# A planned attention and gated-MLP kernel: weight conversion in PSUM, staggered units, and drawn visit orders

## Chip, cores and metric

One core of one Trainium2 chip. The metric is the device time of one execution in microseconds, the median of several runs. Five engines matter: PE (TensorE), DVE (VectorE), ACT (ScalarE), POOL (GpSimd) and SP, which issues the DMAs. PEld is the weight load of PE.

## The reference

Attention for 8 batches of 8 heads, 576 tokens, head size 64, in which only scores close to the row's maximum count, and behind it a gated MLP on 4608 tokens:

```python
scores = scale * np.matmul(q, k.transpose(0, 1, 3, 2))
thresh = np.max(scores, axis=-1, keepdims=True) - tau
scores = np.where(scores >= thresh, scores, -1000000000.0)
attn = np.exp(scores - np.max(scores, axis=-1, keepdims=True))
attn = attn / (np.sum(attn, axis=-1, keepdims=True) + 1e-09)
x = np.matmul(attn, v)                 # to 4608 x 512, all fp32
gate = 1.0 / (1.0 + np.exp(-(x @ w_gate)))
out = (gate * (x @ w_val)) @ w_out     # d_ff 1536
```

## The kernel before

**A planner writes the order.** The program records operations (`Plan.op`: engine, cost, key, what is read and written). `Plan.run` then plays them with these costs: on each free engine it starts the ready operation with the smallest key for which buffers are free, and emits instructions in the order so found. Each engine runs its list in that order; nothing is reordered on the chip. The costs decide the order and nothing else.

**Attention.** 32 visits, one for each batch and pair of heads (named 0_0 to 7_3). A visit has nine score tiles of 128 rows. For each (`tile_steps`): PE writes 128x576 scores into PSUM (L623, two row halves of the array at once), DVE takes the row maximum (L630), ACT the exponential (L644), DVE masks and sums (L647), PE transposes (L738, `Group.transpose`), ACT copies the transposed tile to SBUF (L686). `outputs` multiplies by V (L777, column halves of the array).

**PSUM.** Eight banks, shared out by the planner (`PLACES`, `SLOTS`). A buffer of tag "s" takes a pair of banks: scores, transposes, leftover keys, V products. A buffer of tag "b" takes one bank: accumulators of the MLP. Once the MLP runs beside attention, "s" buffers are kept to three pairs (`homes`), and at most two accumulators are alive (`MOE_CAP`).

**Weights.** `convert` is called 36 times for 128x512 pieces. A piece arrives as pairs of 32-bit words and becomes one fp32 word and then a rounded high and a low part: POOL keeps the sign bits (L497, `wa`), ACT scales the magnitude (L501, `wb`), DVE shifts and joins `wb` with `wa` (L504), DVE joins the low word with `wb` (L510), ACT rounds (L522), POOL subtracts (L528). `wb` is one SBUF buffer (tag "cv", one slot).

**MLP.** Block 0 (batch 0) runs with the whole array (`whole_units`, L888). Blocks 1 and 2 (batches 1 and 2) run in `in_units`: for each of 12 column tiles f the accumulators of the gate (i = 0) and of the value (i = 1) are summed together, one on array rows 0 to 63 and the other on rows 64 to 127 (`phase`, L848), and then with the rows exchanged. Between the two phases ACT reads one element of an accumulator (`seen`, L857), which keeps both row halves from adding to one bank at once. After the second phase ACT takes tanh (L956) and DVE forms the product (L961). Then come `out_pair` (L848 again, operands `gpp`, prepared on ACT, POOL and DVE) and, once the attention's buffers are free, three rounds of `in_two` (L1179) and `out_two` (L1321) for the other six blocks, with the whole array.

Of the kernel before, what the change touches and what calls it, by code (L numbers as in the profile page):

```python
# [10 lines left out]
F32 = mybir.dt.float32  # L11
# [32 lines left out]
class Plan:  # L44
# [5 lines left out]
    def __init__(self, pools, slots):  # L50
        self.pools, self.slots = pools, slots
        self.ops, self.held, self.made, self.given = [], {}, {}, {}
        self.live = {}

    def buf(self, tag, shape, dtype, name, cls=None):
        return Buf(self, tag, shape, dtype, name, cls)
# [9 lines left out]
    def op(self, eng, cost, key, emit, reads=(), writes=(), also=(), leave=0, behind=None, after=(), lag=0.0, mode="full"):  # L66


        o = Op()
        o.eng, o.cost, o.emit, o.key, o.leave, o.lag = eng, cost, emit, key, leave, lag  # L70
        o.succ, o.seq, o.ready, o.mode = [], len(self.ops), 0.0, mode
        deps, bufs = set(after), []
        for group, write in ((reads, False), (writes, True)):
            for x in group:
                b, part = x if isinstance(x, tuple) else (x, None)
                for q, p, w in b.accesses:
                    if (write or w) and (p is None or part is None or p == part):
# [18 lines left out]
        return o  # L96

# [145 lines left out]
    "p": 4, "pc": 1, "sm": 8, "st": 8, "cv": 1, "pt": 5, "pl": 3, "ptc": 1, "xf": 2, "rb": 1, "x": 6, "g": 12,  # L243
# [75 lines left out]
YIELD = -1  # L319
# [23 lines left out]
def kernel(  # L343
# [80 lines left out]
    class Both(Plan):  # L424
        def cap(self, tag, cls):
# [4 lines left out]
            if cls in ("conv", "chain"):  # L430
                return 1 if active["att"] else None
# [38 lines left out]

    def convert(i, f, key):
# [13 lines left out]
        def load():  # L485
# [10 lines left out]
        bt = buf("cv", [P, DM], F32, f"wb{name}")  # L496
        op("POOL", 0.8, key, lambda: nc.gpsimd.tensor_scalar(  # L497
# [3 lines left out]
        op("ACT", 0.67, key, lambda: nc.scalar.activation(bt.ap, hi().bitcast(F32), AF.Abs, scale=2.0**-112),  # L501
           reads=[raw], writes=[bt])
        a = lambda: bt.ap.bitcast(I32)
        op("DVE", 0.69, key, lambda: nc.vector.scalar_tensor_tensor(  # L504
            out=a(), in0=a(), scalar=3, in1=at.ap, op0=ALU.logical_shift_left, op1=ALU.bitwise_or
        ), reads=[at], writes=[bt])

        lo_by_dve = LO_DVE(f if i == 2 else 2 * f + i, i == 2)
        res = bt if lo_by_dve else at
        op("DVE", 0.69, key, lambda: nc.vector.scalar_tensor_tensor(  # L510
            out=res.ap.bitcast(I32), in0=lo(), scalar=29, in1=a(), op0=ALU.logical_shift_right, op1=ALU.bitwise_or
        ), reads=[raw, bt], writes=[res])
# [29 lines left out]

    class Part:


        def __init__(self, b, get, part=None):
            self.b, self.get, self.part = b, get, part

    class Visit:
# [28 lines left out]
        def plain_scores(self, key, n):  # L578
# [16 lines left out]
            for h in range(2):  # L595
                for j, (c0, c1) in enumerate(pieces if h == 0 else [(0, SK)]):
# [6 lines left out]
                    op("POOL", 0.83, key + h, lambda h=h, c0=c0, c1=c1: nc.gpsimd.tensor_scalar(  # L603
# [86 lines left out]
    class Group:  # L690
# [19 lines left out]
        def normalise(self, key):  # L710
# [4 lines left out]
            for i in range(n):  # L715
                op("POOL", 0.9, key, lambda i=i: nc.gpsimd.tensor_scalar(
# [144 lines left out]

    last_load = [None]
# [61 lines left out]
    def in_units(blk, xs, g, c0, c1, c0x, weights):  # L924
# [3 lines left out]
        W = c1 - c0  # L928
        held = {}
        for f in [f + z for f in F1 for z in (0, 2)] if blk in SUMS_IN else range(NF):  # L930
            th = buf("t2", [P, W], F32, f"th{blk}_{f}")
            items = []
            for i in range(2):
                m = buf("b", [P, W], F32, f"m{blk}_{f}_{i}", "moe")
                w = held[f, i] = weights(f, i)
                wv = lambda w=w: w.ap if len(w.shape) == 3 else w.ap.rearrange("p (z f) -> p z f", z=2)
                mms = [(
                    lambda wv=wv, a=a, c=c: wv()[:, a, c * P : (c + 1) * P], lambda c=c, z=z: xs[c].ap[:, z, c0:c1],
                    e == 0, e == 11, [xs[c], w],
                ) for e, (c, a, z) in enumerate((c, a, z) for c in range(ND) for a, z in ((0, 0), (0, 1), (1, 0)))]  # L940
                items.append((mms, m))
            for r in range(2):
                whole = items
                if r:
                    whole = [([(a, b, False, d, e) for a, b, _, d, e in mms], m) for mms, m in items]
                else:
                    whole = [([(a, b, c, False, e) for a, b, c, _, e in mms], m) for mms, m in items]
                end = phase(whole, r, not r, [g[f], th] if r else ())
                unit_ends.append(end)
                begun.setdefault(blk, end)  # L950
            for i in range(2):
                m = items[i][1]
                if f not in F1 and i in SUMS_IN.get(blk, ()):
                    in_sums(f - 2, i, held[f - 2, i], held[f, i])
                if i == 0:
                    op("ACT", act(W), YIELD if blk in OUT_PAIR else -1, lambda m=m, th=th: nc.scalar.activation(  # L956
                        th.ap, m.ap, AF.Tanh, scale=0.5
                    ), reads=[m], writes=[th])
                elif blk in OUT_PAIR:
                    z = OUT_PAIR.index(blk)  # L960
                    op("DVE", dve(W), YIELD, lambda m=m, th=th, f=f, z=z: nc.vector.scalar_tensor_tensor(  # L961
                        out=g[f].ap[:, z], in0=th.ap, scalar=1.0, in1=m.ap, op0=ALU.add, op1=ALU.mult
                    ), reads=[m, th], writes=[(g[f], z)])
                else:
                    op("DVE", dve(W), -1, lambda m=m, th=th: nc.vector.scalar_tensor_tensor(
                        out=th.ap, in0=th.ap, scalar=1.0, in1=m.ap, op0=ALU.add, op1=ALU.mult
                    ), reads=[m], writes=[th])
                    hi = lambda f=f: g[f].ap[:, 0, c0:c1]
                    op("ACT", act(W), -1, lambda th=th, hi=hi: nc.scalar.copy(hi(), th.ap),
                       reads=[th], writes=[(g[f], (0, c0))])  # L970
                    op("POOL", pool(W), -1, lambda th=th, hi=hi, f=f: nc.gpsimd.tensor_tensor(
                        out=g[f].ap[:, 1, c0:c1], in0=th.ap, in1=f32(hi()), op=ALU.subtract
                    ), reads=[th, (g[f], (0, c0))], writes=[(g[f], (1, c0))])
# [447 lines left out]
    def attention(vis):  # L1421
        paired = PAIRED(vis.b, vis.hp)
        vis.prepare(LEAD)
        t, groups = vis.first, []
        for h, tiles in vis.groups:
# [6 lines left out]
            g.transpose(t - 0.5)  # L1432
# [137 lines left out]
```

## Time and profile before

| | us |
|---|---|
| median of 3 runs (1343.67 to 1345.08) | 1344.76 |
| the profiled execution, its own time | 1344.47 |
| its span in the trace | 1342.6 |
| PE busy, share of the span | 1279.0, 95% |
| DVE busy | 918.1, 68% |
| ACT busy | 684.9, 51% |
| POOL busy | 526.7, 39% |

The time is some 1.9 us above the span. The work falls into three stretches: to about 175 us attention, weight conversion and the first half of block 0; to about 828 us attention beside blocks 0 to 2; then the six other blocks, on PE alone. Busy PE is not PE at its peak: two row halves at once show as two matmuls, and switches of the array's tiling are inside busy time.

### The profile page before, as it was taken

The page shows a single profiled execution, that of the slowest core. Times are in us where ns is not written, and L with a number is a line of the kernel's source. Part 1 is how long each engine was busy: PE and PEld are TensorE (multiplying, and loading weights), DVE is VectorE, ACT ScalarE, POOL GpSimd, SP SyncE. Part 2 cuts the span into 40 slices and gives each one's busy share as a digit, 9 for nine tenths or more (in the row PEclk, how much of TensorE's full clock was granted, in tenths as well). Part 3 has the DMA queues.
Part 4 walks back from the last instruction along what each step waited for, and adds up shares of the span by engine and source line. Part 5 has one row for each costly group of instructions (what it writes and reads, how often), then busy time and mean ns, then how long its engine had stood idle before and what let it go on. Part 6 is the DMA issues. An engine that isn't in the chain of part 4 may idle for free.

```text
span 1342.6 us, 27594 instructions
## 1 busy us (share of the span) xinstructions
PE 1279.0 (95%) x10596; PEld 1004.7 (75%) x10596; DVE 918.1 (68%) x1811; ACT 684.9 (51%) x1120; POOL 526.7 (39%) x501
## 2 busy tenths in 40 slices
PE   7778899999999999999999989999999999999998
PEld 5545566778777777777777767888888888888887
DVE  7889987666677767676767743556955569654594
ACT  6776666667566656676666642224531235322242
POOL 4686765757333437677347551110001010001100
PEclk9889999999999999999999999999999999999999
DMA  8668756678656657786644577766686566766663
GB/s 296 201 240 291 252 204 195 208 251 275 203 181 197 204 195 277 243 299 234 209 146 146 182 255 259 251 189 203 211 291 198 190 206 199 245 187 199 195 204 122
DMA packets 134571, 293.17 MB, mean 218 GB/s; under 512 B 27304, under 2 KB 62376, under 8 KB 134440
## 3 DMA queue, kind: packets, MB, share of 16 engines
q1 hardware_dynamic: 134296, 291.41, 65.8%
q8 instruction: 84, 1.38, 0.4%
q14 instruction: 47, 0.39, 0.1%
q10 hardware_dynamic: 144, 0.00, 0.0%
HBM read 229.34 MB, written 62.01 MB: 217 GB/s over the span
## 4 chain that ended last, share of the span: by engine, by line
PE 84%; DVE 7%; ACT 3%; issue 2%; POOL 2%; DMA 2%; SPq 0%; DVEq 0%; ACTq 0%; POOLq 0%
PE banks L1179 26%; PE banks L848 16%; PE banks L1321 13%; PE banks L623 11%; PE banks L777 10%; PE banks L738 6%; PE banks L888 3%; DVE p L647 2%; DVE wa L510 2%; DVE wb L504 1%; DVE st L630 1%; ACT pt L686 1%; DMA wr<-in_moe_w_out_dram 1%; ACT p L644 1%; DMA xa<-xa 0%
## 5 line engine op out<-in xcount | busy, mean ns | idle before, releaser
L630 DVE TENSOR_REDUCE st<-banks 128x1 f32<-128x576 f32 x256 | 190.9, 751 | 135.0 <-PE banks L623 131.6
L623 PE MATMUL banks<-kp,qp 64*128 64x288 f32 x1280 | 213.2, 435 | 29.8 <-DVE p L647 17.0
L647 DVE SCALAR_TENSOR_TENSOR p<-banks,st,p 128x576 f32<-128x576 f32 x256 | 205.9, 812 | 28.5 <-ACT p L644 21.9
L644 ACT ACTIVATE p<-banks,st 128x576 f32<-128x576 f32 x256 | 187.4, 745 | 36.4 <-DVE st L630 33.6
L848 PE MATMUL banks<-x,wi 64*128 64x512 f32 x1152 | 187.7, 431 | 5.4 <-DVE g L961 4.2
L1092 POOL TENSOR_TENSOR gA<-gA 128x512 f32<-128x512 f32 x18 | 24.2, 1347 | 426.6 <-DVE gA L1158 426.6
L623 PEld LDWEIGHTS banks<-kp,qp 64*128 64x128 f32 x1280 | 119.1, 194 | 72.9 <-DVE p L647 28.2
L1321 PE MATMUL banks<-gs_p,wo_p 128*128 128x512 f32 x756 | 172.3, 389 | 0.0
L1321 PEld LDWEIGHTS banks<-gs_p,wo_p 128*128 128x128 f32 x756 | 141.9, 188 | 29.5
L686 ACT COPY pt<-banks 128x1024 f32<-128x1024 f32 x128 | 129.6, 1013 | 48.5 <-PE banks L738 45.5
L738 PEld LDWEIGHTS banks<-ident,p 64*128 64x128 f32 x2304 | 102.7, 141 | 43.1 <-DVE p L647 9.5
L848 PEld LDWEIGHTS banks<-x,wi 64*128 64x128 f32 x1152 | 111.3, 186 | 25.6 <-DVE g L961 6.7
L777 PE MATMUL banks<-pt,vs 128*64 128x256 f32 x1024 | 123.2, 383 | 5.7 <-ACT pt L686 4.1
L738 PE MATMUL banks<-ident,p 64*128 64x64 f32 x2304 | 111.7, 227 | 12.1 <-ACT pl L686 5.4
L1116 DVE TENSOR_TENSOR qu<-banks,qp 128x512 f32<-128x512 f32 x72 | 49.8, 692 | 102.6 <-PE banks L1179 62.6
L1179 PE MATMUL banks<-xs_p,wa 128*128 128x512 f32 x432 | 111.0, 393 | 0.0
L1179 PE MATMUL banks<-xs_p,wt 128*128 128x512 f32 x432 | 109.5, 389 | 0.0
L1179 PE MATMUL banks<-xs_p,ws 128*128 128x512 f32 x432 | 104.4, 390 | 0.0
L777 PEld LDWEIGHTS banks<-pt,vs 128*64 128x64 f32 x1024 | 69.3, 137 | 45.3 <-ACT pt L686 7.1
L1179 PEld LDWEIGHTS banks<-xs_p,wa 128*128 128x128 f32 x432 | 81.7, 190 | 18.0 <-issue 1.0
L1179 PEld LDWEIGHTS banks<-xs_p,ws 128*128 128x128 f32 x432 | 80.9, 188 | 17.4 <-issue 0.7
L1179 PEld LDWEIGHTS banks<-xs_p,wt 128*128 128x128 f32 x432 | 81.1, 188 | 16.8
(124 smaller groups left out, 2037.2 us busy)
## 6 DMA issues: line engine op xcount, KB each, us to landing
wi<-wid SPq DMA_DIRECT2D x48, 512.0 KB
qp<-in_q_dram SPq DMA_DIRECT2D x31, 640.0 KB
wa<-wid SPq DMA_DIRECT2D x36, 512.0 KB
ws<-sid SPq DMA_DIRECT2D x36, 512.0 KB
wt<-sid SPq DMA_DIRECT2D x36, 512.0 KB
wo_p<-sod SPq DMA_DIRECT2D x36, 512.0 KB
wo_p<-wod SPq DMA_DIRECT2D x27, 512.0 KB
vs<-in_v_dram SPq DMA_DIRECT2D x32, 384.0 KB
```

The lines of the kernel that those rows point to most:

```text
L623: nc.tensor.matmul(s.ap[:, c, :HALF], vis.q1.ap[rows, x, c0 : c0 + P], vis.k1[x].ap[rows, kc : kc + HALF], start=x == heads[0][0], stop=x ...
L630: op("DVE", 0.76, key, lambda: nc.vector.tensor_reduce(out=st.ap[:, 0:1], in_=sv(), axis=AX.XY, op=ALU.max, negate=True), reads=[s], write ...
L644: op("ACT", 0.74, key, lambda: nc.scalar.activation(p(), sv(), AF.Exp, bias=st.ap[:, 0:1], scale=1.0), reads=[s, (st, 0)], writes=[(g.p, i)])
L647: mask = op("DVE", 0.9, key, lambda: nc.vector.scalar_tensor_tensor(out=p(), in0=sv(), scalar=st.ap[:, 1:2], in1=p(), op0=ALU.is_ge, op1=A ...
L686: op("ACT", act(n), key, lambda: nc.scalar.copy(dst(), src()), reads=at, writes=[part])
L738: nc.tensor.matmul(banks[z]()[:, m * D : (m + 1) * D], p.ap[rows, o : o + P], ident[rows, rows], is_transpose=True, start=m == 0, stop=m = ...
L777: nc.tensor.matmul(av.get()[h * D : (h + 1) * D, a:z], vis.vs.ap[:, j, h], m(h), start=i == 0, stop=i == len(ms) - 1, skip_group_check=True,)
L848: nc.tensor.matmul(acc.ap, w()[h], x()[h], start=start, stop=stop, skip_group_check=True)
L888: nc.tensor.matmul(m.ap, wv[:, a, c * P : (c + 1) * P], xs[c].ap[:, z, c0:c1], start=e == 0, stop=e == 11,)
L1116: f = lambda: nc.vector.tensor_tensor(out=out.ap, in0=ps_[bank].ap, in1=x.ap, op=ALU.add)
L1179: nc.tensor.matmul(acc.ap, wv[:, y, (2 * h + c) * P : (2 * h + c + 1) * P], xt[prod][c].get()[:, z], start=e == 0 and prod in FIRST, stop= ...
L1321: nc.tensor.matmul(acc.ap, w.ap[:, e, c, y], gt[prod][2 * g + c].get()[:, z], start=m == 0 and g == 0 and prod in FIRST, stop=m == 5 and g ...
```

## The change

Six edits, in one:

1. `convert` puts `wb` into a PSUM pair (tag "s", class "c", at most one alive) in place of the SBUF buffer. The result of both joins is `wa`, in SBUF, as before.
2. `in_units` no longer sums gate and value together. `staggered` runs 24 units (f, i) in a row; while a unit is on rows 0 to 63, the one before it is on rows 64 to 127. There is one `seen` for each unit (48 in place of 24). The first step of a block and its last have a single unit on the array.
3. V products may take any free pair of banks, the fourth too.
4. While a visit is recorded, each key below 398 gets a random amount between -3 and 3, from a seed per visit (`ORDERS`; 0: none).
5. A group's transposes get key t - 1 in place of t - 0.5; block 0 takes six matmuls at a time in place of four.
6. Five of the planner's costs are set anew.

```diff
-    "p": 4, "pc": 1, "sm": 8, "st": 8, "cv": 1, "pt": 5, ...
+    "p": 4, "pc": 1, "sm": 8, "st": 8, "pt": 5, ...
-STAY, SWITCH, TURN = 4, 0.15, 0.06
+STAY, SWITCH, TURN = 4, 0.15, 0.0615
-MM_HALVES = 0.2265
-WHOLE, FULL_STEP = (0,), 4
+MM_HALVES = 0.234
+WHOLE, FULL_STEP = (0,), 6
+ORDERED, NUDGE = 398, 3.0
+ORDERS = (
+    9752, 0, 748, 1675, 6489, 1465, 5011, 3559, 9165, 5460, 4071, 9213, 3320, 7371, 6555, 4493,
...
+        if 0 <= key < ORDERED:
+            key += self.nudge()
...
-            if cls in ("conv", "chain"):
+            if cls == "c":
+                return 1
+            if cls == "chain":
                 return 1 if active["att"] else None
...
-            return at[:3] if b.tag == "s" and active["moe"] and active["att"] else at
+            return at[:3] if b.tag == "s" and b.cls != "av" and active["moe"] and active["att"] else at
...
-        bt = buf("cv", [P, DM], F32, f"wb{name}")
-        op("POOL", 0.8, key, lambda: nc.gpsimd.tensor_scalar(
+        bp = buf("s", [P, 2, SM], F32, f"wb{name}", "c")
+        bt = Part(bp, lambda: bp.ap[:, 0])
+        op("POOL", 0.92, key, lambda: nc.gpsimd.tensor_scalar(
...
-        res = bt if lo_by_dve else at
+        res = at
...
-                    op("POOL", 0.83, key + h, lambda h=h, c0=c0, c1=c1: nc.gpsimd.tensor_scalar(
+                    op("POOL", 0.89, key + h, lambda h=h, c0=c0, c1=c1: nc.gpsimd.tensor_scalar(
...
-                op("POOL", 0.9, key, lambda i=i: nc.gpsimd.tensor_scalar(
+                op("POOL", 1.12, key, lambda i=i: nc.gpsimd.tensor_scalar(
...
+    def staggered(units, step=2):
+        before = None
+        for make in units + [None]:
+            now = make() if make else None
+            pair = [(u, z) for u, z in ((now, 0), (before, 1)) if u]
+            n = len(pair[0][0][0])
+            for at in range(0, n, step):
+                def go(at=at, pair=pair):
+                    for e in range(at, min(at + step, n)):
+                        for (mms, acc, _, _), z in pair:
+                            w, x, _ = mms[e]
+                            nc.tensor.matmul(
+                                acc.ap, w()[ROWS[z]], x()[ROWS[z]], start=e == 0 and z == 0, stop=e == n - 1 and z == 1,
+                                skip_group_check=True,
+                            )
...
+            if now:
+                op("ACT", 0.2, -2, lambda acc=now[1]: nc.scalar.copy(seen, acc.ap[0:1, 0:1]), reads=[now[1]])
+            if before:
+                before[3]()
...
-            g.transpose(t - 0.5)
+            g.transpose(t - 1)
```

Both programs have the same instructions apart from 24 more `seen` copies on ACT. Three places show how they are moved; `banks` is PSUM.

DVE in visit 1_0 (rows whose tiles begin `0_` there), where most conversions lie; L504 and L510 are L528 and L534 in the change, L630 and L647 are L648 and L665. Before:

```order
L639 TENSOR_SCALAR st_0_001_1288<-st_0_001_1288,ntau_t 128x1
L639 TENSOR_SCALAR st_0_l_1217<-st_0_l_1217,ntau_t 128x1
L504 SCALAR_TENSOR_TENSOR wb_1_1309<-wb_1_1309,wa_1_958 128x512
L510 SCALAR_TENSOR_TENSOR wa_1_958<-wr_1_878,wb_1_1309 128x512
L647 SCALAR_TENSOR_TENSOR p_0_00_1311,sums_130<-banks,st_0_000_1262,p_0_00_1311 128x576
L504 SCALAR_TENSOR_TENSOR wb_2_1322<-wb_2_1322,wa_2_1186 128x512
L795 TENSOR_TENSOR x_3_1325<-banks,x_3_1325 128x256
L510 SCALAR_TENSOR_TENSOR wa_2_1186<-wr_2_1066,wb_2_1322 128x512
```

In the change:

```order
L665 SCALAR_TENSOR_TENSOR p_0_00_1266,sums_130<-banks,st_0_001_1218,p_0_00_1266 128x576
L813 TENSOR_TENSOR x_3_1297<-banks,x_3_1297 128x256
L528 SCALAR_TENSOR_TENSOR banks<-banks,wa_1_707 128x512
L534 SCALAR_TENSOR_TENSOR wa_1_707<-wr_1_649,banks 128x512
L648 TENSOR_REDUCE st_0_020_1333<-banks 128x1
L813 TENSOR_TENSOR x_3_1297<-banks,x_3_1297 128x256
L528 SCALAR_TENSOR_TENSOR banks<-banks,wa_0_846 128x512
L534 SCALAR_TENSOR_TENSOR wa_0_846<-wr_0_765,banks 128x512
```

Each join had two SBUF operands and now has one in PSUM, and the two joins of a piece stand side by side.

PE in block 1, where one unit follows another (`wi_f_i` are weights; i = 0 gate, 1 value). L623 is L641 and L848 is L892 in the change. Before, from f = 2 to f = 1:

```order
L848 MATMUL banks<-x_3_3025,wi_2_1_3996 128x512
L848 MATMUL banks<-x_3_3025,wi_2_0_3959 128x512
L623 MATMUL banks<-kp_1_0_3640,qp_1_3730 128x288 x2
L848 MATMUL banks<-x_0_2017,wi_1_0_4157 128x512
L848 MATMUL banks<-x_0_2017,wi_1_1_4159 128x512
```

In the change, from the step with 3_1 and 3_0 to the step with 4_0 and 3_1:

```order
L892 MATMUL banks<-x_3_3060,wi_3_1_4216 128x512
L892 MATMUL banks<-x_3_3060,wi_3_0_4140 128x512
L641 MATMUL banks<-kp_1_1_3888,qp_1_3880 128x288 x4
L892 MATMUL banks<-x_0_1914,wi_4_0_4391 128x512
L892 MATMUL banks<-x_0_1914,wi_3_1_4216 128x512
```

Before, both accumulators end together and two new ones begin; now one ends and one begins at each step, with about as much attention work between.

PE at the end of the last visit's V products; L777 is L795, L848 of `out_pair` is L866, L1179 is L1213. Before:

```order
L777 MATMUL banks<-pt_3_l_10641,vs_3_9932 64x64 x10
L848 MATMUL banks<-gpp_2_10678,wpair_p_1_10351 128x512 x2
L848 MATMUL banks<-gpp_3_10698,wpair_p_1_10351 128x512 x6
L848 MATMUL banks<-gpp_4_10709,wpair_p_2_10359 128x512 x6
L848 MATMUL banks<-gpp_5_10718,wpair_p_2_10359 128x512 x6
L848 MATMUL banks<-gpp_0_10839,wpair_p_0_10655 128x512 x6
```

In the change:

```order
L795 MATMUL banks<-pt_3_l_10895,vs_3_10180 64x64 x10
L866 MATMUL banks<-gpp_1_10672,wpair_p_0_10402 128x512 x4
L866 MATMUL banks<-gpp_2_10693,wpair_p_1_10410 128x512 x6
L866 MATMUL banks<-gpp_3_10717,wpair_p_1_10410 128x512 x6
L866 MATMUL banks<-gpp_4_10769,wpair_p_2_10416 128x512 x6
L866 MATMUL banks<-gpp_5_10774,wpair_p_2_10416 128x512 x6
L1213 MATMUL banks<-xs_p_0_10986,ws_0_0_10432 128x512 x3
```

Before, the last V products are followed by 164 matmuls of blocks 1 and 2 and three products of `in_two` among them; now by 64, and four products of `in_two` stand ahead of the V products.

## Rows read from the trace of the kernel before

**Rows 1.** The page: span, busy time, POOL's busy tenths in 40 slices

```profile
span 1342.6 us, 27594 instructions
PE 1279.0 (95%) x10596; PEld 1004.7 (75%) x10596; DVE 918.1 (68%) x1811; ACT 684.9 (51%) x1120; POOL 526.7 (39%) x501
...
POOL 4686765757333437677347551110001010001100
```

**Rows 2.** Stretches: length, busy PE, PEld, DVE, ACT, POOL, PE clock, DMA share, GB/s

```profile
0.00:47.00 47.00, 34.20 (x330) 24.21 (x332) 35.77 (x74) 31.85 (x49) 23.89 (x43) 0.89 0.81 284
47.00:75.00 28.00, 22.01 (x292) 16.09 (x290) 24.37 (x46) 22.07 (x36) 16.77 (x24) 0.94 0.55 185
75.00:105.00 30.00, 18.47 (x198) 12.46 (x194) 27.06 (x48) 18.89 (x32) 27.35 (x28) 0.89 0.73 244
105.00:175.00 70.00, 62.16 (x428) 41.06 (x428) 66.70 (x107) 46.40 (x78) 49.27 (x40) 0.98 0.79 270
320.00:800.00 480.00, 463.94 (x5494) 365.17 (x5492) 334.49 (x815) 307.43 (x500) 255.91 (x234) 1.00 0.64 213
800.00:830.00 30.00, 24.98 (x161) 17.99 (x158) 7.46 (x12) 4.62 (x9) 9.91 (x8) 0.89 0.72 240
```

**Rows 3.** The chain that ended last by line: whole span, then 100 to 190 us

```profile
by line: PE banks L1179 25.7%; PE banks L848 15.7%; PE banks L1321 12.8%; PE banks L623 10.7%; PE banks L777 10.4%; PE banks L738 5.7%; PE banks L888 3.2%; issue 2.4%; DVE p L647 1.9%; DVE wa L510 1.5%; DVE wb L504 1.4%; DVE st L630 1.2%; A
...
by line: PE banks L888 18.1%; DVE wa L510 14.7%; DVE wb L504 10.4%; DMA wr<-in_moe_w_out_dram 10.0%; PE banks L623 9.8%; issue 6.7%; DVE p L647 6.1%; PE banks L777 5.6%; DMA rb<-rd 3.4%; POOL ws L528 2.9%; PE banks L738 2.9%; DVE st L630 1.
```

**Rows 4.** Groups of instructions, 0 to 175 us: both joins of the conversion

```profile
L510 DVE SCALAR_TENSOR_TENSOR wa<-wr,wb 128x512 int32<-128x512 int32 x30 | 38.2, 1272 | 0.9
...
L504 DVE SCALAR_TENSOR_TENSOR wb<-wb,wa 128x512 int32<-128x512 int32 x30 | 29.4, 979 | 4.1 <-ACT wb L501 3.4
```

**Rows 5.** Other DVE rows: L647 alone (min/median/max), then groups, whole span

```profile
L647 DVE SCALAR_TENSOR_TENSOR p<-banks,st,p x256: 776/814/820, 8.4 to 787.9; 128x576 f32<-128x576 f32 x128
...
L961 DVE SCALAR_TENSOR_TENSOR g<-th,banks 128x512 f32<-128x512 f32 x24 | 16.4, 681 | 1.5 <-ACT th L956 1.3
...
L1092 DVE TENSOR_TENSOR gA<-gB,gA 128x512 f32<-128x512 f32 x18 | 11.6, 681 | 0.1
```

**Rows 6.** Waits, 0 to 175 us (total, times, longest), and ACT's part of a conversion

```profile
ACT wb L501 <- DVE wa L510: 19.3, 14, 2.3
...
PE banks L623 <- DVE p L647: 12.9, 13, 2.7
...
PE banks L623 <- ACT pt_l L686: 3.4, 2, 2.6
...
L501 ACT ACTIVATE wb<-wr 128x512 f32<-128x512 f32 x36 | 24.3, 674 | 19.7 <-DVE wa L510 19.3 <-DMA wr<-in_moe_w_gate_dram 0.4
```

**Rows 7.** Pieces of the chain: start, length, matmuls of L888, L1179 and L848

```profile
105.10 1.18 PE banks L888 x4
...
185.00 3.85 PE banks L888 x16
...
807.46 2.86 PE banks L1179 x6
...
814.13 8.39 PE banks L848 x72
...
828.41 107.69 PE banks L1179 x474
```

**Rows 8.** ACT groups of the units, and what PE's L848 sat idle for, whole span

```profile
L956 ACT ACTIVATE th<-banks 128x512 f32<-128x512 f32 x24 | 14.3, 596 | 6.4 <-PE banks L848 6.3
...
L857 ACT COPY seen<-banks 1x1 f32<-1x1 f32 x37 | 5.4, 146 | 19.9 <-PE banks L848 19.6
...
  DVE g L961: 10.9, 12
...
  ACT seen L857: 3.9, 10
```

**Rows 9.** Waits, 800 to 830 us

```profile
PE banks L848 <- POOL gpp L1087: 5.0, 1, 5.0
```

More of the change, by code (lines that the diff above doesn't have):

```diff
@@ L2 @@
 import itertools
+import random
 from contextlib import ExitStack
@@ L53, in __init__ @@
         self.live = {}
+        self.nudge = lambda: 0.0
     def buf(self, tag, shape, dtype, name, cls=None):
@@ L96, in op, with vary @@
         return o
+    def vary(self, seed):
+        draw = random.Random(seed)
+        self.nudge = (lambda: draw.uniform(-NUDGE, NUDGE)) if seed else lambda: 0.0
     def room(self, o):
@@ L469, with __init__ @@
         nc.vector.memset(sm.t, 1.0)
+    class Part:
+        def __init__(self, b, get, part=None):
+            self.b, self.get, self.part = b, get, part
     def convert(i, f, key):
@@ L500, in convert @@
         ), reads=[raw], writes=[at])
-        op("ACT", 0.67, key, lambda: nc.scalar.activation(bt.ap, hi().bitcast(F32), AF.Abs, scale=2.0**-112),
-           reads=[raw], writes=[bt])
-        a = lambda: bt.ap.bitcast(I32)
+        op("ACT", 0.67, key, lambda: nc.scalar.activation(bt.get(), hi().bitcast(F32), AF.Abs, scale=2.0**-112),
+           reads=[raw], writes=[bp])
+        a = lambda: bt.get().bitcast(I32)
         op("DVE", 0.69, key, lambda: nc.vector.scalar_tensor_tensor(
             out=a(), in0=a(), scalar=3, in1=at.ap, op0=ALU.logical_shift_left, op1=ALU.bitwise_or
-        ), reads=[at], writes=[bt])
+        ), reads=[at], writes=[bp])
         lo_by_dve = LO_DVE(f if i == 2 else 2 * f + i, i == 2)
-        res = bt if lo_by_dve else at
+        res = at
         op("DVE", 0.69, key, lambda: nc.vector.scalar_tensor_tensor(
             out=res.ap.bitcast(I32), in0=lo(), scalar=29, in1=a(), op0=ALU.logical_shift_right, op1=ALU.bitwise_or
-        ), reads=[raw, bt], writes=[res])
+        ), reads=[raw, bp], writes=[res])
         if i == 2:
@@ L540, in convert @@
             ), reads=[ws], writes=[(wo_d[f // ND], f)])
-    class Part:
-        def __init__(self, b, get, part=None):
-            self.b, self.get, self.part = b, get, part
     class Visit:
@@ L860 @@
     unit_ends, begun, xs = [], {}, {}
+    def staggered(units, step=2):
[12 more added lines that the diff above has]
+                                skip_group_check=True,
+                            )
+                rd = list(dict.fromkeys(y for (mms, *_), _ in pair for m in mms[at : at + step] for y in m[2]))
+                also = [b for (_, _, more, _), z in pair if z for b in more]
+                end = last_phase[0] = moe_pe(
+                    min(step, n - at) * MM_HALVES, go, rd, [acc for (_, acc, *_), _ in pair], also=also,
+                    after=[last_phase[0]] if last_phase[0] else (), mode="row",
+                )
+            if now:
+                op("ACT", 0.2, -2, lambda acc=now[1]: nc.scalar.copy(seen, acc.ap[0:1, 0:1]), reads=[now[1]])
+            if before:
+                before[3]()
+            unit_ends.append(end)
+            before = now
+        unit_ends.pop()
     last_load = [None]
@@ L927, in in_units @@
             return whole_units(blk, xs, g, c0, c1, c0x, weights)
[L928 to L945, printed above, removed]
-                else:
[L947 to L961, printed above, removed]
@@ new lines, in in_units, with unit, done @@
+        held, ths = {}, {}
+        def unit(f, i):
+            if i == 0:
+                ths[f] = buf("t2", [P, SM], F32, f"th{blk}_{f}")
+            th = ths[f]
+            m = buf("b", [P, SM], F32, f"m{blk}_{f}_{i}", "moe")
+            w = held[f, i] = weights(f, i)
+            wv = lambda: w.ap if len(w.shape) == 3 else w.ap.rearrange("p (z f) -> p z f", z=2)
+            mms = [(
+                lambda a=a, c=c: wv()[:, a, c * P : (c + 1) * P], lambda c=c, z=z: xs[c].ap[:, z, c0:c1], [xs[c], w],
+            ) for c in range(ND) for a, z in ((0, 0), (0, 1), (1, 0))]
+            z = OUT_PAIR.index(blk)
+            def done():
+                if f not in F1 and i in SUMS_IN.get(blk, ()):
+                    in_sums(f - 2, i, held[f - 2, i], w)
+                if i == 0:
+                    op("ACT", act(SM), -1, lambda: nc.scalar.activation(th.ap, m.ap, AF.Tanh, scale=0.5),
+                       reads=[m], writes=[th])
+                else:
+                    op("DVE", dve(SM), -1, lambda: nc.vector.scalar_tensor_tensor(
@@ L962, in in_units @@
                         out=g[f].ap[:, z], in0=th.ap, scalar=1.0, in1=m.ap, op0=ALU.add, op1=ALU.mult
                     ), reads=[m, th], writes=[(g[f], z)])
[L964 to L973, printed above, removed]
+            return mms, m, [g[f]] if i else [th], done
@@ L975, in out_units @@
+        fs = [f + z for f in F1 for z in (0, 2)] if blk in SUMS_IN else range(NF)
+        at = len(unit_ends)
+        staggered([lambda f=f, i=i: unit(f, i) for f in fs for i in range(2)])
+        begun[blk] = unit_ends[at]
     def out_units(blk, g):
@@ L1421, in attention @@
     def attention(vis):
+        plan.vary(ORDERS[4 * vis.b + vis.hp])
         paired = PAIRED(vis.b, vis.hp)
```

3 lines of the change are left out of this document (2 added, 1 removed).

## The prediction

> **What bounds the kernel now.** I read the page first, then the span cut into stretches, then the chain of waits, then single rows where a term needs a price. The page says that PE is busy for 1279.0 of 1342.6 us [rows 1], so at most 63.6 us can be won without taking work off PE. The stretches show where they lie: before 175 us PE is idle for 12.8, 6.0, 11.5 and 7.8 us, 38.2 in all; from 320 to 800 us for 16.1; from 800 to 830 us for 5.0 [rows 2]. Before 175 us the busy engine is DVE: 153.9 us of 175, and 66.7 of the 70 from 105 on. After that PE is full and DVE is not. So a thing that DVE does counts early, and a thing that PE does counts late.
>
> The chain of waits confirms it. Over the span the two joins of the conversion, L510 and L504, lie on it with 1.5% and 1.4%, that is 0.029 x 1342.6 = 38.9 us; from 100 to 190 us they are 25.1% of it [rows 3]. The waits name DVE too: PE's largest early wait is 12.9 us for DVE's mask, and ACT stands 19.3 us before it may write the next `wb`, until DVE has read the last [rows 6].
>
> **Conversion in PSUM (edit 1).** Up to 175 us there are 30 of each join, of 1272 and 979 ns, 67.6 us together [rows 4]. Operations of the same 512 columns take 681 ns, with an operand in PSUM (L961) or with none (L1092) [rows 5]. What makes the joins slow is POOL beside them: L1092's are in the last stretch, where POOL is busy for a tenth or less [rows 1]. An operation that reads one operand from PSUM is not slowed by POOL: the mask L647 reads PSUM and SBUF, runs 256 times, most of them beside a busy POOL, and its longest is 820 ns against a median of 814 [rows 5]. After the edit both joins read one operand from PSUM and one from SBUF. I take 0.69 us each: DVE's work before 175 us falls by 67.6 - 60 x 0.69 = 26.2 us. What of it ends up in the time is read from the chain. The mean of the 60 joins is 67.6 / 60 = 1.126 us, so the 38.9 us on it shrink by 1 - 0.69 / 1.126 = 39%: **-15.1 us**. Ends: 0, if something else is late at once, and 26.2, if DVE alone sets the pace. The first join also writes PSUM, and ACT writes `wb` there; the trace has neither. Nearest are DVE and ACT reading PSUM at no extra cost [rows 5, 8], so I take none.
>
> The Trainium skill (Perfetto Trace Analysis, Optimizing Scalar/DVE Operations) puts a DVE access to PSUM at about 125 ns against 60 in SBUF, and ACT's at 51 against 93. By it the 60 joins would give back an estimated 60 x 65 ns = 3.9 us of DVE's 26.2, and the term would fall by some 2 us. The rows with PSUM (681) and without (681) do not show that difference, so the sum goes without it.
>
> What is late next is a pair of banks. A conversion holds one from ACT's start to DVE's second join: at least 0.67 + 2 x 0.69 = 2.1 us [rows 6], so 36 of them hold one of four pairs for 75 us or more of the first 220. PE already waits for evictions at times (3.4 us for ACT's L686 copies is the largest [rows 6]). I leave this at nothing, because DVE frees pairs sooner too, and keep it as a rival.
>
> **Units staggered (edit 2).** The 1152 matmuls stay. A pair of row halves is cheap: 72 matmuls of L848 take 8.39 us on the chain, 0.117 each, while whole-array ones take 107.69 / 474 = 0.227 [rows 7]. In each of the two blocks the first and the last step have a single unit, 2 x 2 x 12 = 48 matmuls that run alone. The trace has no such one. It cannot cost less than its half of a pair (term 0) and hardly more than a whole-array one, which streams the same 512 columns; I take the latter: 48 x (0.227 - 0.117) = **+5.3 us**.
>
> Between steps PE must wait for an eviction. Before, it waited mostly where a new f begins, since both banks come free only after tanh and product: 10.9 us on L961, and 3.9 on `seen` [rows 8]. Now each of 48 steps waits for one eviction (0.60 or 0.68 us) with `seen` (0.15) ahead of it, and the order puts 0.3 to 1.2 us of attention between most steps. Half the wait at twice the places: I take 0, with ends of -14.8 (all gone) and +23 (below). The 24 new `seen` cost ACT 24 x 0.146 = 3.5 us, covered: from 320 to 800 us ACT is busy 307 of 480 us [rows 2]; were it not, they would show as part of that wait.
>
> **Order (edits 3 to 6).** PE changes between whole array, row halves and column halves 161 times before, 143 after, counted in the two orders. A visit of four matmuls of L888 takes 1.18 us, one of 16 takes 3.85 [rows 7]; less 0.227 each, 0.27 and 0.22 remain for two changes, about 0.12 each: 18 x 0.12 = **-2.2 us** (ends 0 and -2.4). At the end of attention PE stands idle for 5.0 us before the change, waiting for a `gpp` on POOL [rows 9], and six matmuls of L1179 behind that gap take 2.86 us, where 6 x 0.227 = 1.36 would do [rows 7], with the granted clock at 0.89 in that stretch [rows 2]: 6.5 us. In the new order blocks 1 and 2 run ahead of attention by 100 matmuls there, with part of `in_two` before the last V products, so POOL's chain has cover. But attention's last visit then has less other work beside it. I take half, **-3.2 us**; ends 0 and -6.5. V products on a fourth pair and earlier transposes remove no instruction; their gain, if any, is in the idle 16.1 us of the middle, and I take none.
>
> **The sum**, against the profiled execution's own 1344.47 us (0.3 below the median shown): 1344.5 - 15.1 + 5.3 - 2.2 - 3.2 = **1329.3 us**.
>
> **Rivals.**
> *A, larger gain.* DVE alone set the early pace, and the tail gap closes whole: 1329.3 - (26.2 - 15.1) - 3.3 = 1315. For it: PE's early idle is 38.2 us and DVE is 95% busy from 105 on. Against it: DMA is busy at 0.79 there, and a load of weights lies on that chain with 10.0% [rows 3].
> *B, the pair of banks.* The early gain goes into waits for a free pair: 1329.3 + 15.1 = 1344. For it: the pair is held in the stretch where MLP and attention meet, with three pairs left. Against it: evictions account for little of PE's early waits.
> *C, the change does not do what it says.* The joins stay slow beside POOL although one operand is in PSUM, or a write to PSUM makes up for it: also 1344. Against it: L647's 820 ns.
> *D, the tail.* Its gap stays, and the shorter cover leaves `in_two` waiting for attention's buffers to be refilled: 1329.3 + 3.2 + 4.4 = 1337, the 4.4 us being two loads of 512 KB at the 240 GB/s of that stretch [rows 2].
> *E, slower.* PE finds nothing to do at the 48 steps and each shows its eviction whole: 48 x (0.64 + 0.15) = 37.9 us in place of 14.8, so +23 and 1352. It decides if cover falls under some 0.3 us per step. The `seen` waits, 3.9 us in this trace [rows 8], now stand at twice as many places. The Trainium skill (TensorEngine Tiling (Array Packing), Restrictions and Gotchas) names why they exist: different row tiles may not access one PSUM bank at once, and software has to see to it. Against the rival: the order has row work between most steps.
>
> **How the numbers follow.** Forecast 0.50 (its own range 1321 to 1337), A 0.16, B 0.11, C 0.04, D 0.11, E 0.08. Differences under 0.2%, 2.7 us, can hardly be told from none. Faster: forecast, A, D and about half of B and C, 0.84; same: the other half, 0.07; slower: E and a little of B, 0.09. The range runs from short of A's 1315 to the near side of B, 1313 to 1343; beyond it lie E and half of B and C above, and something below A.
>
> **What would show it.** Right, if both joins run near 0.69 us with POOL busy, DVE's work before the first block's end is some 26 us less, PE's early idle falls from 38 to about 23 us, and the wait for `gpp` is gone or halved. The lone steps should show 48 matmuls about 0.22 us apart. Wrong, if the joins keep over 0.9 us, if PE's early waits move from DVE's mask to evictions, or if L892 (now the unit's matmul) sits idle much over 15 us for `seen`, tanh and product.

## The result and the profile after

The change takes **1306.75 us** (median of 4 runs, 1304.2 to 1309.39) against 1344.86 for the kernel before: ratio 0.972, 95% interval 0.970 to 0.974. The forecast was 1329.3 with a range of 1313 to 1343: the direction is right, the gain is 38 us in place of 15. The profiled execution has 1305.66 us.

The page of the change, its span, its busy times, and POOL's busy tenths [rows 1]:

```profile
span 1303.6 us, 27638 instructions
...
PE 1265.9 (97%) x10596; PEld 997.8 (77%) x10596; DVE 892.8 (68%) x1811; ACT 685.4 (53%) x1144; POOL 512.8 (39%) x501
...
POOL 4567777665444366584868400111001100010100
```

PE is idle for 1303.6 - 1265.9 = 37.7 us, where it was 63.6. DVE does 25.3 us less work. The stretches, with the columns of [rows 2]:

```profile
0.00:47.00 47.00, 35.61 (x378) 25.13 (x378) 35.15 (x78) 33.58 (x52) 22.91 (x45) 0.93 0.72 258
47.00:75.00 28.00, 20.54 (x278) 14.78 (x276) 24.15 (x52) 21.95 (x35) 16.71 (x28) 1.00 0.63 204
75.00:105.00 30.00, 27.24 (x226) 19.30 (x227) 23.93 (x52) 21.12 (x36) 20.06 (x21) 0.83 0.76 247
105.00:175.00 70.00, 69.82 (x542) 49.06 (x542) 56.55 (x116) 53.46 (x87) 51.42 (x49) 1.00 0.87 301
...
320.00:800.00 480.00, 471.23 (x5439) 369.69 (x5440) 335.55 (x806) 302.63 (x516) 250.70 (x225) 1.00 0.67 222
800.00:830.00 30.00, 29.21 (x129) 23.86 (x128) 14.75 (x22) 6.66 (x11) 5.18 (x4) 1.00 0.77 272
```

Idle of PE before 175 us falls from 38.2 to 21.8 us, most of it from 75 us on. From 320 to 800 us it falls from 16.1 to 8.8 us. The joins of the conversion, 0 to 175 us [rows 4]:

```profile
L528 DVE SCALAR_TENSOR_TENSOR banks<-banks,wa 128x512 int32<-128x512 int32 x30 | 20.8, 692 | 1.4 <-ACT banks L525 0.8 <-POOL wa L521 0.3
L534 DVE SCALAR_TENSOR_TENSOR wa<-wr,banks 128x512 int32<-128x512 int32 x30 | 20.6, 686 | 0.9
```

Both joins run at 0.69 us with POOL busy beside them. ACT's part of a conversion, whole span [rows 6], waits less for the second join:

```profile
L525 ACT ACTIVATE banks<-wr 128x512 f32<-128x512 f32 x36 | 23.2, 647 | 7.0 <-DVE wa L534 5.8 <-DVE p L665 0.4 <-DVE p_l L665 0.3
```

At the end of attention the chain goes from work to work, where the kernel before had 5.0 us of waiting for `gpp` [rows 9] (start, length, what):

```profile
776.36 5.06 PE banks L795 x68
781.42 3.44 PE banks L866 x28
784.86 1.59 PE banks L1213 x6
786.45 4.30 PE banks L866 x36
790.75 16.58 PE banks L1213 x72
```

The six matmuls of L1213 take 1.59 us; the six of L1179 took 2.86 [rows 7]. The last row-half matmul starts at 790.4 us (before: 828.0). From there to the last matmul it is 510 us before and 509 in the change. So nearly all of the gain lies ahead of this point, called the hand-over below.

**One table for all runs.** From the matmuls' starts in each trace I added up, until the hand-over, the *gaps*: where two matmuls in a row start over 0.55 us apart, the first of them at full clock, the distance less 0.22 us. "Early" is before 175 us, "late" from 320 us on (between them 0.4 to 6.1 us). The last column is the time that PE ran at half clock. Times are medians; the kernel before ran beside each group at 1344.0 to 1344.9 us.

```text
run                                    us     ratio [95%]               early  late  half clock
before                                 1344.9                            37.2  24.1   27.9
the change                             1306.8 0.972 [0.970, 0.974]       18.1   9.4   16.8
a  wb in SBUF, order of the change     1322.2 0.984 [0.983, 0.986]       32.8  10.2   19.1
b  no draws                            1331.2 0.991 [0.990, 0.993]       24.1  22.6   19.8
m  wb in SBUF, order of b              1348.4 1.003 [1.002, 1.004]       38.1  24.2   30.7
e  seeds + 1                           1347.8 1.003 [1.002, 1.004]       24.0  27.8   36.9
f  seeds + 20000                       1329.9 0.990 [0.988, 0.992]       22.8  18.5   16.3
k  seeds + 40000                       1338.4 0.995 [0.993, 0.997]       22.2  24.0   32.4
i  draws for 8 visits                  1330.6 0.990 [0.988, 0.992]       21.4  26.6   16.8
j  draws for 16 visits                 1321.2 0.982 [0.979, 0.984]       18.8  20.0   23.7
c  no staggering                       1322.3 0.984 [0.982, 0.986]       19.2  22.7   22.9
g  no staggering, no draws             1337.0 0.994 [0.993, 0.996]       22.2  31.2   24.6
d  before + conversion in PSUM         1337.8 0.996 [0.994, 0.997]       27.3  23.4   30.0
h  before + draws                      1344.0 1.000 [0.999, 1.001]       31.5  25.1   31.8
```

Two things can be read at once. The early column follows edit 1: 31 to 38 us with `wb` in SBUF, 18 to 27 with it in PSUM. The late column is 9 to 10 us only in the change and in *a*, which has its order, and 18 to 31 us in every other order.

### The profile page after: what moved, and what is told of

Same layout as the page of the kernel before. It is cut to its first block, busy times and chain, and to the rows that moved or that the text cites. A ratio compares the mean times of both kernels' runs of the same rounds, so it can differ in the third digit from the quotient of the medians.

```text
span 1303.6 us, 27638 instructions
## 1 busy us (share of the span) xinstructions
PE 1265.9 (97%) x10596; PEld 997.8 (77%) x10596; DVE 892.8 (68%) x1811; ACT 685.4 (53%) x1144; POOL 512.8 (39%) x501
## 4 chain that ended last, share of the span: by engine, by line
PE 86%; DMA 3%; DVE 3%; POOL 2%; ACT 2%; issue 2%; SPq 1%; DVEq 0%; POOLq 0%; ACTq 0%
PE banks L1213 26%; PE banks L1355 13%; PE banks L795 11%; PE banks L892 11%; PE banks L641 10%; PE banks L756 5%; PE banks L866 5%; PE banks L937 4%; DMA rb<-rd 1%; DVE p L665 1%; ACT pt L704 1%; DMA xa<-xf 1%; DVE st L648 1%; DMA sod<-s_o 0%; DMA qp<-in_q_dram 0%
## 5 line engine op out<-in xcount | busy, mean ns | idle before, releaser
L648 DVE TENSOR_REDUCE st<-banks 128x1 f32<-128x576 f32 x256 | 190.3, 753 | 142.3 <-PE banks L641 136.5
L665 DVE SCALAR_TENSOR_TENSOR p<-banks,st,p 128x576 f32<-128x576 f32 x256 | 205.0, 813 | 25.2 <-ACT p L662 18.3
L641 PE MATMUL banks<-kp,qp 64*128 64x288 f32 x1280 | 204.2, 424 | 12.9 <-DVE p L665 6.5
L892 PE MATMUL banks<-x,wi 64*128 64x512 f32 x1152 | 178.6, 423 | 3.5 <-DVE g L998 2.5
L641 PEld LDWEIGHTS banks<-kp,qp 64*128 64x128 f32 x1280 | 113.5, 189 | 49.7 <-DVE p L665 14.5
L892 PEld LDWEIGHTS banks<-x,wi 64*128 64x128 f32 x1152 | 111.3, 186 | 25.9 <-DVE g L998 5.1
L795 PE MATMUL banks<-pt,vs 128*64 128x256 f32 x1024 | 124.7, 386 | 5.6 <-DVE p L665 3.9
L756 PEld LDWEIGHTS banks<-ident,p 64*128 64x128 f32 x2304 | 98.2, 141 | 35.3 <-DVE p L665 5.1
L756 PE MATMUL banks<-ident,p 64*128 64x64 f32 x2304 | 106.1, 227 | 6.1 <-DVE p L665 2.6
L1213 PE MATMUL banks<-xs_p,wa 128*128 128x512 f32 x432 | 110.2, 390 | 0.0
L1213 PE MATMUL banks<-xs_p,wt 128*128 128x512 f32 x432 | 109.2, 389 | 0.0
L795 PEld LDWEIGHTS banks<-pt,vs 128*64 128x64 f32 x1024 | 69.9, 138 | 47.2 <-DVE p L665 5.9
L1213 PE MATMUL banks<-xs_p,ws 128*128 128x512 f32 x432 | 104.1, 390 | 0.0
L1213 PEld LDWEIGHTS banks<-xs_p,wa 128*128 128x128 f32 x432 | 80.8, 188 | 17.8 <-issue 1.2
L1213 PEld LDWEIGHTS banks<-xs_p,ws 128*128 128x128 f32 x432 | 80.9, 188 | 17.5 <-issue 0.7
L1213 PEld LDWEIGHTS banks<-xs_p,wt 128*128 128x128 f32 x432 | 81.1, 188 | 16.9
```

The costliest lines, as they stand in the source:

```text
L641: nc.tensor.matmul(s.ap[:, c, :HALF], vis.q1.ap[rows, x, c0 : c0 + P], vis.k1[x].ap[rows, kc : kc + HALF], start=x == heads[0][0], stop=x ...
L648: op("DVE", 0.76, key, lambda: nc.vector.tensor_reduce(out=st.ap[:, 0:1], in_=sv(), axis=AX.XY, op=ALU.max, negate=True), reads=[s], write ...
L665: mask = op("DVE", 0.9, key, lambda: nc.vector.scalar_tensor_tensor(out=p(), in0=sv(), scalar=st.ap[:, 1:2], in1=p(), op0=ALU.is_ge, op1=A ...
L756: nc.tensor.matmul(banks[z]()[:, m * D : (m + 1) * D], p.ap[rows, o : o + P], ident[rows, rows], is_transpose=True, start=m == 0, stop=m = ...
L795: nc.tensor.matmul(av.get()[h * D : (h + 1) * D, a:z], vis.vs.ap[:, j, h], m(h), start=i == 0, stop=i == len(ms) - 1, skip_group_check=True,)
L892: nc.tensor.matmul(acc.ap, w()[ROWS[z]], x()[ROWS[z]], start=e == 0 and z == 0, stop=e == n - 1 and z == 1, skip_group_check=True,)
```

## The experiments

### a: wb back in SBUF, every engine's list unchanged

```diff
-        bt = Part(bp, lambda: bp.ap[:, 0])
+        held = []
+        def place():
+            if not held:
+                bp.ap
+                held.append(sb.tile([P, DM], F32, tag="cv", name=f"wb{name}", bufs=1))
+            return held[0]
+        bt = Part(bp, place)
```

The planner still reserves the pair of banks, so it writes the same order; the pair is only not used.

> The changed kernel with exactly its order of instructions on every engine, but with wb in an SBUF buffer again (the pair of banks stays reserved and unused). Theory 1 (what wins early is the price of the two joins beside POOL): the joins go back to about 1.1 us, PE's idle before 175 us rises from 22 to 35 us or more, and the time is about 1320 to 1325, some 15 us over the change. Theory 2 (the win is in the order, the joins were covered): the joins slow down too, but the time stays within 4 us of the change's 1307.

Measured 1322.15 us, 15.4 above the change. The joins in this run, 0 to 175 us:

```profile
L542 DVE SCALAR_TENSOR_TENSOR wa<-wr,wb 128x512 int32<-128x512 int32 x29 | 33.9, 1169 | 0.9
L536 DVE SCALAR_TENSOR_TENSOR wb<-wb,wa 128x512 int32<-128x512 int32 x29 | 26.4, 909 | 1.9 <-ACT wb L533 0.6 <-POOL wa L529 0.6
```

and the stretch of 105 to 175 us:

```profile
105.00:175.00 70.00, 61.45 (x426) 43.31 (x426) 64.76 (x96) 45.87 (x77) 60.18 (x44) 0.98 0.82 280
```

PE is idle here for 8.6 us, in the change for 0.2, and DVE is busy for 64.8 in place of 56.6. With nothing moved, the place of `wb` is worth 15.4 us. My term was 15.1. The pair of banks is reserved in both kernels, so what it costs is not in this number.

### b: no draws

```diff
-ORDERS = (
-    9752, 0, 748, 1675, 6489, 1465, 5011, 3559, 9165, 5460, 4071, 9213, 3320, 7371, 6555, 4493,
-    0, 1253, 2636, 4108, 9865, 7590, 738, 2276, 1215, 1549, 3530, 2072, 647, 565, 5179, 0,
-)
+ORDERS = (0,) * 32
```

> The changed kernel with all 32 seeds at 0, so the order within visits is by the plain keys. Theory 1 (conversion and staggering carry the gain): within 4 us of the change, 1303 to 1311. Theory 2 (the draws closed PE's waits in the middle, 23 to 9 us, and part of the early ones): 1318 to 1326, with PE's waits over 0.55 us back at 45 us or more in total.

Measured 1331.19 us, 5 us above the range of theory 2: the draws are worth 24.4 us, and without them the kernel stands 2 us from my forecast. The middle stretch of this run, then of the change:

```profile
320.00:770.00 450.00, 431.48 (x5067) 335.52 (x5066) 313.88 (x768) 286.40 (x486) 241.34 (x220) 1.00 0.63 206
```

```profile
320.00:770.00 450.00, 442.81 (x5206) 348.22 (x5206) 320.01 (x775) 296.65 (x505) 249.27 (x224) 1.00 0.66 218
```

Idle of 18.5 us against 7.2. What PE and PEld sat idle for ahead of the units' matmuls (L889 in *b*, L892 in the change), whole span, first *b*:

```profile
  DVE g L995: 17.9, 32
  ACT th L992: 10.6, 22
```

```profile
  DVE g L998: 7.5, 17
  ACT th L995: 4.0, 11
```

Without draws the steps between units wait 28.5 us for the evictions, with them 11.5. The kernel before had 15.7 by this view [rows 8, the 0.9 us for tanh counted in], 0.9 of it for `seen` ahead of `out_pair`. The view adds the idle time of PE and of PEld, which can be the same time twice. PE's own waits there, before, in *b* and in the change:

```profile
PE banks L848 <- DVE g L961: 4.2, 5, 1.2
...
PE banks L848 <- ACT seen L857: 1.1, 4, 0.4
```

```profile
PE banks L889 <- DVE g L995: 6.6, 15, 0.8
...
PE banks L889 <- ACT th L992: 2.9, 9, 0.7
```

```profile
PE banks L892 <- DVE g L998: 2.5, 6, 0.8
...
PE banks L892 <- ACT th L995: 1.0, 3, 0.5
```

That is 5.3, 9.5 and 3.5 us. So rival E's mechanism is there in an order that was not chosen, with some 4 us in place of its +23, and in the order of the listed draws it is covered. These waits explain 6 of the 24.4 us. By the table the late gaps are 13.2 us apart, early ones 6.0, and the half-clock time 3.0 (worth half of it); the late gaps that do not lie between units are mostly ahead of `out_pair` (5.4 us in *b*, 1.6 in the change, from the same starts) and of attention's matmuls.

### m: wb in SBUF, order of b

The edits of *a* and *b* together.

> The change without draws, every engine's list the same as in that run, but the conversion's middle value back in an SBUF buffer (the pair of banks is still reserved, and unused). In the change's own drawn order the same edit cost 15.4 us (1322.2 against 1306.8). Theory 1 (the 15 us are the joins' own time on the chain, whatever the order): 1331.2 + 12 to 18 = 1343 to 1349; then the small gain of the conversion alone in the kernel before (6.4 us) is 15 less a worse order. Theory 2 (an order that was not chosen hides much of the joins behind other waits, and the 15 us belong to the chosen order): 1331 to 1339.

Measured 1348.37 us, 17.2 above *b*. Joins, 0 to 175 us:

```profile
L539 DVE SCALAR_TENSOR_TENSOR wa<-wr,wb 128x512 int32<-128x512 int32 x29 | 34.4, 1187 | 0.9
L533 DVE SCALAR_TENSOR_TENSOR wb<-wb,wa 128x512 int32<-128x512 int32 x29 | 28.8, 993 | 4.6 <-POOL wa L526 2.3 <-ACT wb L530 0.9 <-POOL ws L557 0.3
```

The price of the joins' operand is 15 to 17 us in two orders that differ by 24 us. It belongs to the joins, not to the chosen order.

### d: the kernel before with edit 1 alone

```diff
-        bt = buf("cv", [P, DM], F32, f"wb{name}")
+        bp = buf("s", [P, 2, SM], F32, f"wb{name}", "c")
+        bt = Part(bp, lambda: bp.ap[:, 0])
...
+            if cls == "c":
+                return 1
             if cls in ("conv", "chain"):
...
-        res = bt if lo_by_dve else at
+        res = at
```

> The kernel before with edit 1 alone: wb in a pair of PSUM banks, all else as it was, costs included. Theory 1 (price of the joins): -15 us, 1330. Theory 2 (the pair it takes costs as much as it gives): 1340 to 1346. Theory 3 (edit 1 is most of the gain): 1320 or less.

Measured 1337.77 us, ratio 0.996: 6 to 7 us, not 15, and between theories 1 and 2. The planner writes another order as soon as a buffer moves, so this run is edit 1 and a new order in one. Its early gaps fall by 9.9 us, where the joins' operand alone gives 14.7 [*a*] and 14.0 [*m*] of early gaps. Its late ones stay (23.4, the 5.0 us for `gpp` among them), and those in between grow by 2.2 us. Whether the missing part of the 15 us went to the new order or to the pair of banks stays open; waits of PE that end with the join that frees the pair are 0.8 us here.

### e, f, k: other draws

Every nonzero seed raised by 1, by 20000, by 40000:

```diff
-    9752, 0, 748, 1675, 6489, 1465, 5011, ...
+    9753, 0, 749, 1676, 6490, 1466, 5012, ...
```

> The change with every nonzero seed raised by 1: same spread of draws, other draws, in all visits. Theory 1 (the draws are worth something because these particular ones fit this plan): the 24 us that separate the change (1306.8) from the change without draws (1331.2) go, time 1326 to 1345, and the hand-over to the last stretch stands later by the same amount. Theory 2 (any scatter of the keys loosens the order, for instance by breaking ties between visits): most of the 24 us stay, 1305 to 1316.

> The change with every nonzero seed raised by 20000, a second independent set of draws. Theory 1 (these particular draws): 1326 to 1345. Theory 2 (any draws): 1305 to 1316. The two sets together also show how far a time scatters from the order alone: by theory 1 they may differ from each other by 5 us or more, with the same instructions.

> The change with every nonzero seed raised by 40000, a third set that nobody chose. The first two gave 1347.8 and 1329.9, no draws 1331.2. If the scatter of orders that were not chosen is centred on the plan without draws: 1325 to 1348, and the change's 1306.8 stays the lowest of all by over 15 us. If draws are as likely to help as not by 20 us: 1305 to 1325.

Measured 1347.83, 1329.91 and 1338.38 us. With *b* that makes four orders which nobody chose, of the same instructions: 1329.9 to 1347.8, 18 us apart, all at least 23 us above the change. Run *e* is 3 us beyond even the range of theory 1. Draws as such win 1 us at best and lose up to 17 against *b*; the listed ones fit this plan. How they were found is not on record. Run *e* shows what a bad one does. Its wait at the end of attention, and the stretch around it:

```profile
PE banks L863 <- POOL gpp L1118: 8.1, 1, 8.1
```

```profile
800.00:830.00 30.00, 21.90 (x146) 15.76 (x144) 7.69 (x12) 6.56 (x14) 10.03 (x8) 0.83 0.65 213
```

It is the wait that the kernel before had with 5.0 us [rows 9]. PE is idle for 8.1 us of these 30, and the granted clock is 0.83 there.

### h: the kernel before with the draws alone

```diff
+        if 0 <= key < ORDERED:
+            key += self.nudge()
...
+        plan.vary(ORDERS[4 * vis.b + vis.hp])
```

> The kernel before with the same draws alone (edit 4). Theory 1 (draws fit one plan): another plan gets nothing or worse, 1342 to 1365. Theory 2 (any scatter helps): a gain of the same kind as in the change, 1320 to 1332.

Measured 1343.98 us, ratio 1.000 [0.999, 1.001]. The draws fit one plan; in another they are any draws.

### i, j: draws for the first 8 and the first 16 visits

```diff
+ORDERS = (9752, 0, 748, 1675, 6489, 1465, 5011, 3559) + (0,) * 24
```

(the second with the first 16 seeds)

> The change with draws for the first 8 visits (batches 0 and 1) alone, none for the other 24. Up to some 175 us the order should be that of the change. Theory 1 (the draws win about as much in the conversion's stretch as later, because idle of PE before 175 us is 18 us of gaps in the change and 24 without draws, with 3 us more of half clock there): 1321 to 1326, some 7 us under the run without draws (1331.2), with idle before 175 us as in the change (21.8 us), and the rest of the 24 us still missing between 320 us and the hand-over. Theory 2 (all is won in the middle, where the gaps past 320 us are 9 us in the change and 23 without draws): 1329 to 1333. Theory 3 (an early order that fits decides the rest too): 1306 to 1312.

> The change with draws for the first 16 visits (batches 0 to 3). Theory 1 (gains add up as the draws go on): between the run with 8 visits drawn and the change, 1311 to 1321. Theory 2 (the middle, by the units of blocks 1 and 2, which lie past 290 us): most of the gain appears only here or later, 1311 to 1329. If the time is above that of the run with 8 visits, single draws have no worth of their own and only the whole set counts: 1325 to 1340.

Measured 1330.56 and 1321.19 us. With 8 visits drawn, three stretches:

```profile
105.00:175.00 70.00, 69.82 (x542) 49.49 (x540) 56.81 (x115) 52.88 (x86) 50.90 (x48) 1.00 0.87 298
...
320.00:770.00 450.00, 432.34 (x4998) 334.34 (x4996) 303.10 (x737) 281.67 (x482) 245.55 (x221) 1.00 0.64 210
770.00:800.00 30.00, 24.03 (x254) 16.92 (x250) 20.62 (x50) 17.77 (x26) 1.40 (x1) 0.96 0.63 201
```

The early stretch is that of the change (542 matmuls in 69.82 us), and the first unit starts at 289.0 us in place of *b*'s 298.7. Yet the time is only 0.6 us under *b*: 17.7 us idle in the middle and 6.0 from 770 to 800 us, where the last visit's scores and transposes wait for DVE's masks with few matmuls of the MLP left beside them. By the table the early gaps and the half clock (counted half) are 4.2 us less than in *b*, and the late gaps 4.0 more. This was my theory 1 for the cause and theory 2 for the time: the early gain is real, and in this order the later stretches give it back. With 16 visits drawn 10 us are won, with all of them 24.

### c, g: the units of before in the change, with and without draws

```diff
-        staggered([lambda f=f, i=i: unit(f, i) for f in fs for i in range(2)])
...
+            for r in range(2):
...
+                end = phase(whole, r, not r, [g[f], th] if r else ())
```

> The changed kernel with blocks 1 and 2 summed as before (gate and value together, rows exchanged after a phase). It loses the 48 lone matmuls (-5.3 us) and takes the waits for both evictions again (+9.5 us by the waits between unit matmuls in the two traces). Theory 1 (staggering is worth the difference): 1309 to 1313. Theory 2 (the draws were fitted to staggered units, and any other plan with these seeds is worse): 1318 or more. Theory 3 (staggering cost more than it gave): 1302.

> The change with the paired units of before and without any draw; beside the run without draws (1331.2, staggered units) it gives the staggering's price with no fitted draws on either side. If my +5.3 us for 48 lone matmuls and nothing for the waits between steps holds: 1326 (1322 to 1329). If staggering wins back waits at its steps, as the 15 us between the change and the change with paired units suggest at face value: 1337 to 1346. If both are about equal (wins back the 5.3): 1331 within 3.

Measured 1322.27 us with the draws (theory 2), 1336.95 without, at the foot of the range for staggering at its face value. Against the change and against *b* staggering is worth 15.5 and 5.8 us. Neither can be taken for its price: the planner orders both anew, the draws were found for the staggered plan, and both numbers are below the 18 us by which orders of one program differ. In *g* the units' waits for product, tanh and `seen` are 9.3 + 5.4 + 0.2 = 14.9 us (PE and PEld together), half of *b*'s, though *g* is the slower. What staggering alone brings stays open.

## Why the prediction was right or wrong

**Conversion in PSUM: the price of the operand's place right, that of the whole edit open.** Foretold -15.1 us, with joins near 0.69 us and 26 us less work for DVE; measured 15.4 [*a*] and 17.2 [*m*], 0.692 and 0.686 us, and 25.3 us. Taking 39% off the joins' share of the chain gave the number here: all of DVE's saving would have been 26, and nothing 0. PE's idle before 175 us, foretold at about 23 us, is 21.8 in the change, but 26.3 without the draws. The further cost that the figures of the Trainium skill (Perfetto Trace Analysis, Optimizing Scalar/DVE Operations) would add for PSUM does not show: 692 and 686 ns with PSUM, 681 without [rows 5].

Rival C falls. Rival B's mechanism is there and small. *a* and *m* keep the pair of banks reserved and do not price it, but waits of PE that end with the join that frees this pair can be read. PE has none in the change; in *b*, 0 to 830 us, they are 3.5 us:

```profile
PE banks L753 <- DVE wa L531: 2.5, 1, 2.5
...
PE banks L638 <- DVE wa L531: 1.0, 1, 1.0
```

One argument against B was misread: that evictions account for little of PE's early waits. Score matmuls read `kp` and `qp` alone, so their 12.9 us for the mask [rows 6], the last reader of a pair of scores, are waits for banks too. In the change they are 5.6 us.

**48 lone matmuls: right.** The first step of block 1 in the change (start, length, count):

```profile
290.92 2.80 PE L892 MATMUL banks<-x,wi 64*128 64x512 f32 x11
```

Behind the first, they start 0.224 to 0.236 us apart, as whole-array ones do, while a pair takes some 0.23 us for two. The last steps of both blocks show the same distances. So the price of +5.3 us stands.

**Switches: about right.** -2.2 us foretold for 161 to 143. Distances of 0.28 to 0.55 us between starts, where the switches and short waits lie, sum to 1.7 us less.

**Tail: half too small.** The wait for `gpp` falls from 5.0 to 0.4 us, and no half clock is left in 800 to 830 us. I took 3.2 of 6.5 us, fearing for the last visit's cover. That fear was sound for other orders (*e* waits 8.1 us, *i* has 6.0 us idle there), and the order of the change shows four products of L1213 ahead of the last V products. I read that in the order and did not trust it.

**The step that failed: "V products on a fourth pair and earlier transposes remove no instruction; their gain, if any, is in the idle 16.1 us of the middle, and I take none."** The draws (edit 4) had no term at all. They are worth 24.4 us [*b*], and the forecast describes the kernel without them: 1329.3 against 1331.2. That this agrees to 2 us is partly luck: orders of the same instructions that nobody chose lie 18 us apart, and in *b* the waits between units cost some 4 us that I had put at nothing. The draws too remove no instruction; they remove gaps, late ones from 22.6 to 9.4 us and early ones from 24.1 to 18.1. Two errors are in the sentence. The order could win more than the 16.1 us, since early idle was open to it as well; of 38.2 us I had let edit 1 take 15 and left the rest alone. And I asked what the edits do as such, where the diff lists 29 seeds: an order with fixed numbers in it is one order, whose time has to be read from its own rows. Rival A came nearest, 8 us above the measured time, but in the main for a wrong reason: at its 1315 us DVE's whole 26 us were to be won, where *a* and *m* show 15 to 17. Its other part, that the tail gap closes, came true.

**Waits between steps: 0 foretold; by PE's own waits +4 us in an order not chosen, -2 in this one** (9.5 and 3.5 against 5.3 us). The 14.8 us of the prediction, and with it the ends of -14.8 and +23, counted PE and PEld both [rows 8] and were too wide. Rival E was a live mechanism of a smaller size; the listed draws avoid it.

How the rest divides among edits 3, 5 and 6 was not tried one by one. All three together, without draws and staggering, are *g* against *d*: -0.8 us, which says nothing beside a scatter of 18.

## What to carry to other kernels

Where a planner writes the order, an edit's price can be measured only with the order held: keep every engine's list and swap the operand's place alone (15.4 and 17.2 us in two orders), because the same edit with a new order showed 6. What the edit takes elsewhere, here a pair of banks, is then not in the number. Before a few microseconds of such a kernel are credited to an edit, run some orders that nobody chose; here they lay 18 us apart. If a diff fixes an order by numbers, price the idle time that order leaves, stretch by stretch, as a term of its own, since it may be the largest.

## What the runs showed of the hardware that was not expected

The conflict of DVE and POOL costs POOL too, which my sum left out. POOL's groups from 0 to 175 us, first with `wb` in SBUF (*a*), then in the change:

```profile
L560 POOL TENSOR_TENSOR ws<-wa,ws 128x512 fp32r<-128x512 f32 x28 | 40.3, 1443 | 16.5 <-ACT ws L554 11.4 <-DVE st L656 4.8
L529 POOL TENSOR_SCALAR wa<-wr,zero_t 128x512 f32<-128x512 f32 x29 | 28.4, 983 | 1.8 <-DMA wr<-in_moe_w_gate_dram 1.8
```

```profile
L552 POOL TENSOR_TENSOR ws<-wa,ws 128x512 fp32r<-128x512 f32 x30 | 38.5, 1286 | 19.7 <-ACT ws L546 19.4
L521 POOL TENSOR_SCALAR wa<-wr,zero_t 128x512 f32<-128x512 f32 x31 | 25.1, 815 | 5.2 <-DMA wr<-in_moe_w_gate_dram 3.1 <-DMA wr<-in_moe_w_val_dram 2.1
```

With the order the same, POOL's own operations are 157 and 168 ns shorter once the joins read PSUM. The Trainium skill (SBUF — State Buffer, SBUF: two separate sides) says why both sides can lose: DVE with two SBUF inputs and POOL share one pair of ports, which whichever starts first holds for its whole instruction, while the other waits. The runs agree: joins of 1169 and 909 ns become 686 and 692, and POOL's part shrinks with them.

ACT's write of `wb` takes 647 ns into PSUM, where it took 674 into SBUF [rows 6]; I had assumed no difference.
